# Gated linear attention and merged expert branches on one core: order and due times of attention's last steps, half-column state products, and D parts placed beside the second layer

## The chip, the cores and the metric

The kernel runs on one core of one Trainium2 chip. The metric is device time in microseconds of one execution, from the host's inputs in the chip's memory to the outputs there. Smaller is better.

The engines: TensorE (PE; its weight loads are listed apart as PEld) does matrix products and transposes into PSUM banks. VectorE (DVE) and ScalarE (ACT) do element-wise work and empty the banks. GpSimd (POOL) and SyncE (SP) mainly issue transfers here. Each engine runs its own instructions in the order in which they were recorded.

## What is computed

Two steps follow each other. The first is a recurrent attention, for each of 4 batches and 8 heads over 768 steps, with heads of 48:

```python
for t in range(S):
    state = alpha[:, :, t, :, None] * state + np.einsum('bhd,bhe->bhde', k[:, :, t], v[:, :, t])
    y[:, :, t] = np.einsum('bhd,bhde->bhe', q[:, :, t], state)
```

Its output, laid out as 3072 rows of 384, is the input of four expert branches whose results are weighted by normalised probabilities and added:

```python
p = domain_probs / (domain_probs.sum(-1, keepdims=True) + 1e-09)
for e in range(E):                       # E = 4, D = 384, F = 1024
    h = np.maximum(x @ w1[e], 0.0)
    out += p[:, e:e + 1] * (h @ w2[e])
```

All inputs and outputs are float32.

## The kernel before

**Units and groups.** Attention is cut into 24 units: a chunk of 128 time steps (`cb`, six of them) of one batch (`b`, four). Units are collected in groups for the experts: a first group of 2, five of 4, and a last of 2. A group of four is 512 rows of `x`. For each group and expert, the first layer (`up`, eight tiles of hidden units) and then the second (`down`, 128 rows of output a slot) are done. The last two groups take turns expert by expert.

**Precision.** TensorE multiplies float32 slowly, and a rounded form (float32r) faster. From the second group on the first layer, and from the third on both layers, numbers are split into a top part, a low part and a third part that corrects for products of the two. For the hidden layer these are made by `hidden_parts`: ScalarE makes `top`, VectorE `low` (L571), and `make_dif` (L581) the third, called the D part here. Before the change, the D part of a full group's tile is made half at once, in the first layer (columns 0 to 255), and half later: the list `later` is emptied, one piece at every fourth matmul, in the next `down`. The last group's D parts, of 256 columns, all go to `later`.

**The second layer's order.** `down` takes two slots at a time (a half, 48 matmuls). Top and low parts are multiplied first for six tiles, then for the last two, and then the D parts of all eight tiles, slot by slot: matmuls 32 to 47. Partial sums are added to `acc` by VectorE (L649), or ScalarE for the first expert.

**Attention's steps.** `attention(u)` is a generator; each `yield` ends a step. Steps 0 to 2 turn alpha, keys and queries (`tp`) and load those of the next unit. Steps 3 to 10 run down seven levels: `copy_q` (ScalarE copies queries into a block `qb`), `next_q` and `next_k` (decays multiplied on, VectorE). Step 7 has the products of levels 0 to 3 (`sc`, 64 by 64 tiles), whose scores are taken into `near` by masked copies (`take`). Step 11 has the products across a chunk (`far`) and levels 4 and 5. Steps 12 and 13 copy `far` and `near` into `lat` (ScalarE). Then, before the change: step 14 the result (`yps`, tiles of 32 columns, values times `lat` plus queries times the state) copied out for the experts; step 15 the keys turned and copied (`AT`, used as `KB`); step 16 the state products (`sps`), added to the state by VectorE. Units of the last chunk have no keys to turn and no state to keep.

**Order.** The schedule is written by hand: the kernel records experts' work in order, and `advance` adds up planned costs (`cost`) after each tile or matmul. `deal` gives each step of each unit a due time on this planned clock; when the clock passes it, the step is recorded there. A unit is spread over two spaces, so that two units overlap; before the change its 17 steps are equally spaced:

```python
events += [(begin + (end - begin) * (j + 1) / BEATS, u, run) for j in range(BEATS)]
```

A group's units must be done `MARGIN` ahead of its first use. The first two units are placed by lists written out.

**Buffers that matter.** PSUM: tag `w` (turns, yps, sps) and tag `sc` (scores, far) have two buffers each, tag `g` (both layers' sums) four. `near` and `lat` are single tiles that all units share. Four blocks `qb` go round. `dec6`, a decay used in the update of the state, has one buffer.

Of the kernel before, what the change touches and what calls it, by code (L numbers as in the profile page):

```python
# [10 lines left out]
F32 = mybir.dt.float32  # L11
# [9 lines left out]
def kernel(  # L21
# [37 lines left out]
    nc = tc.nc  # L59
# [79 lines left out]
    splitting = []  # L139
    stores = deque()  # L140
    late = deque()
    later = deque()
    shared = {}
    accs = {}

    BEATS = 17
    MARGIN = 6.0
    waiting = deque()
    clock = 0.0
# [118 lines left out]
    def attention(u):  # L268
# [41 lines left out]
        def next_q(li):  # L310
            m = LEVELS[li]
            qv = halves(QT, m)[:, :, :, 1, :]
            dv = halved(decs[li])
            nc.vector.tensor_mul(qv, qv, spread(dv[:, :, :, 0], m))  # L314
            dec = work.tile([P, NP, P // (2 * m)], F32, name=f"dec{li}", bufs=1)
            nc.vector.tensor_mul(dec, dv[:, :, :, 0], dv[:, :, :, 1])
            decs.append(dec)

# [90 lines left out]
        st = sts[b]  # L409
        flat_st = st.rearrange("p a i d -> p a (i d)")  # L410
        flat_v = rv.rearrange("p (a i) d -> p a (i d)", i=2)
        yps = ps.tile([P, KC, P], F32, name="yps", tag="w")
        for c in range(KC):


            if c < 2:
                now = [[(2 * c + j // 2, j % 2, (0, HD + TAIL)[j % 2], 2 * QUAD * (j % 2))
                        for j in range(4)]]
                turns = ([(True, now[0])] if cb > 0 else []) + [(False, now[0])]
            else:  # L420
                turns = [(True, [(p, 0, 0, QUAD) for p in range(NP)])] if cb > 0 else []
                turns += [(False, [(p, i, QUAD + TAIL * i, 0) for p in range(NP)]) for i in range(2)]
            for n, (past, turn) in enumerate(turns):
                for j, (p, i, in_v, in_st) in enumerate(turn):
                    nc.tensor.matmul(  # L425
                        yps[QUAD * j:QUAD * (j + 1), c, :],
                        lhsT=flat_st[:, p, in_st:in_st + QUAD] if past
                        else flat_v[:, p, in_v:in_v + QUAD],
                        rhs=QT[:, p, :] if past else lat[:, 2 * p + i, :],
                        start=(n == 0), stop=(n == len(turns) - 1))  # L430
        gi, slot = place[cb, b]
        if slot == 0:
            if gi == 0:
                xTs[gi] = work.tile([P, 3, KC, NT], F32R, name="xT", bufs=1)
                xraws[gi] = xTs[gi][:, 2].bitcast(F32)
            elif gi < LAST:
                xraws[gi] = work.tile([P, KC, NT], F32, name="x_raw", bufs=1)
            else:
                xraws[gi] = []
        if gi < LAST:  # L440
            nc.scalar.copy(out=xraws[gi][:, :, slot * P:(slot + 1) * P], in_=yps)
        else:

            xraws[gi].append(AT)
            nc.scalar.copy(out=AT[:, :KC, :], in_=yps)
        yield

        if cb < NCB - 1:
            KB = AT
            nc.scalar.copy(out=KB, in_=turned(lambda p: KT[:, p, :]))  # L450
            yield
            sps = ps.tile([P, NP, 2, D], F32, name="sps", tag="w")
            for p in range(NP):
                nc.tensor.matmul(sps[:, p], lhsT=KB[:, p, :], rhs=rv[:, 2 * p:2 * p + 2, :D],  # L454
                                 start=True, stop=True)
            for i in range(2):
                rows = slice(HD * i, HD * (i + 1))
                old, add = st[rows, :, i, :], sps[rows, :, i, :]
                if cb == 0:
                    nc.vector.tensor_copy(out=old, in_=add)  # L460
                else:
                    nc.vector.tensor_mul(old, old, decs[-1][rows].broadcast_to([HD, NP, D]))
                    nc.vector.tensor_add(old, old, add)
# [103 lines left out]
    def hidden_parts(x, parts):  # L567
        top, low, dif = parts
        nc.scalar.activation(out=top, in_=x, func=ACT.Relu, scale=TRIM)  # L569
        yield  # L570
        nc.vector.scalar_tensor_tensor(out=low, in0=x, scalar=0.0, in1=top.bitcast(F32),  # L571
                                       op0=ALU.max, op1=ALU.subtract)

        n = x.shape[-1]
        at = n // 2 if n == NT else 0
        if at:
            make_dif(*(part[:, :at] for part in parts))
        later.append([part[:, at:] for part in parts])

    def make_dif(top, low, dif):  # L580
        nc.vector.scalar_tensor_tensor(out=dif, in0=top.bitcast(F32), scalar=1 / 4096.0,  # L581
# [6 lines left out]
    def down(gi, e, slots, between):  # L588


        first = first_piece(gi, e)
        halves_ = split2(gi, e)
        if slots[0] == 0 and makes[1](gi, e):
            making.extend(split_piece(1, first + k) for k in range(NQ))
        if slots[0] == 0 and makes[0](gi, e) and 0 < e < E - 1:
            making.extend(split_piece(0, first + k) for k in range(2, NQ))
        sums = [[ps.tile([P, DM], F32, name=f"ops{j}", tag="g", bufs=4)
                 for j in range(2 if halves_ else 1)] for _ in slots]

        kinds = [((0, 1), range(FCH - 2)), ((0, 1), range(FCH - 2, FCH)), ((2,), range(FCH))]  # L600
        steps = [(part, i, fc) for parts, tiles in (kinds if halves_ else [((3,), range(FCH))])
                 for part in parts for i in range(len(slots)) for fc in tiles]
        for n, (part, i, fc) in enumerate(steps):
            c, f = divmod(fc, FPQ)
            h = hidden[c][:, :, f, slots[i] * P:(slots[i] + 1) * P]
            advance(cost(1, gi, e) / FCH / (3 if halves_ else 1))
            while between and n >= between[0][0] * len(steps):
                between.popleft()[1]()
            if n == len(steps) // 2:
                background()  # L610
            if later and n % 4 == 3:
                make_dif(*later.popleft())
            if halves_:
                w = wt[1][first + c].rearrange("p t (c d) -> p t c d", d=DM)[:, part, f]
                nc.tensor.matmul(sums[i][part // 2], lhsT=h[:, part], rhs=w,  # L615
                                 start=(fc == 0 and part != 1), stop=(fc == FCH - 1 and part != 0))
            else:
                w = wt[1][first + c].rearrange("p (c d) -> p c d", d=DM)[:, f]
                nc.tensor.matmul(sums[i][0], lhsT=h[:, 2].bitcast(F32), rhs=w,  # L619
                                 start=(fc == 0), stop=(fc == FCH - 1))  # L620
            if part >= 1 and fc == FCH - 1:
                add_up(gi, e, slots[i], part // 2, sums[i][part // 2 if halves_ else 0])
        while between:
            between.popleft()[1]()
        background()
        if slots[-1] == len(groups[gi]) - 1 and gi != LAST - 1:
            while makes[1](gi, e) and (making or splitting):
                background()

            for c in range(NQ):  # L630
                del wt[1][first + c]
                if c < NQ // 2 or gi == LAST:
                    load_piece(1, first + NQ + c)
                else:
                    late.append(first + NQ + c)
# [31 lines left out]
    def deal():  # L667

        wanted = [0.0]
        ends = [0.0, 0.0]
        events = []
        t = 0.0
        for (gi, e), after in zip(tasks, tasks[1:]):
            part = 1 - 1 / len(groups[0]) if gi == e == 0 else 1
            t += cost(0, gi, e) * FCH * part
            if after[1] == 0:
                wanted.append(t)
            t += cost(1, gi, e) * len(groups[gi]) * part  # L680

        for gis in [*([gi] for gi in range(1, LAST - 1)), [LAST - 1, LAST]]:
            gi, due = gis[0], wanted[gis[-1]] - MARGIN
            n = sum(len(groups[i]) for i in gis)
            first = wanted[gi - 1] if gi > 1 else 0.0
            space = (due - first) / (n if gi > 1 else (n + 1) / 2)
            if gi == 1:
                space /= 2
            for k in range(n):
                u = sum(map(len, groups[:gi])) + k  # L690
                end = due - (n - 1 - k) * space
                begin = max(end - 2 * space, ends[-2])
                ends.append(end)
                run = attention(u)
                events += [(begin + (end - begin) * (j + 1) / BEATS, u, run) for j in range(BEATS)]
        return sorted(events, key=lambda x: x[:2])

    def advance(spent):
# [100 lines left out]
```

## Time and profile before

The table is from the profiled execution and from the runs; the page's names are used.

| | |
|---|---|
| median of 12 runs | 1079.52 us (1077.53 to 1081.02) |
| profiled execution, own time | 1082.44 us |
| its span, first to last instruction | 1080.6 us |
| mean granted TensorE clock | 0.993 |
| L615, second layer's split products | 1728 records, 318.5 us busy |
| L531, first layer's split products (`one`, `two`) | 1728 records, `one` of 512 columns 253.6 us |
| L619, second layer in float32 | 384 records, 135.8 us |
| L581, D parts, 128 by 256 | 288, mean 421 ns |
| L333, level products | 2304 records, 77.6 us |
| L425, result | 768 and 480 records, 34.7 and 25.1 us |
| L454, state products, 128 by 96 | 160 records, 21.0 us |
| HBM traffic | 232 GB/s over the span |

A float32 product appears as two records. Lengths of matmul records overlap each other[...]; what a matmul costs is the distance between starts. "Idle before" and the waits' view name what released an engine that had nothing to do. Busy shares are averages over stages with different limits: the first 170 us work in float32, then the split stages with attention follow to about 890 us, and then the last groups without attention.

### The profile page before, as it was taken

The numbers are of one execution on the slowest core, as the hardware profiler recorded it, in microseconds if no ns is written. First come the engines' busy times: TensorE is split into PE (matmuls) and PEld (weight loads), VectorE is DVE, ScalarE is ACT, GpSimd is POOL, SyncE is SP. The second block draws the span as 40 slices with busy tenths as digits, with TensorE's granted clock in tenths as the row PEclk, the third lists the DMA queues.
The fourth block names the chain that finished last, engine by engine and source line by source line (L and its number), as shares of the span: only waits on it lengthen the run. The fifth ranks groups of instructions, "written<-read, shape, count | busy, mean of one in ns | idle before, by whom it ended". The sixth has DMA issues, their size and how long they took to land.

```text
span 1080.6 us, 21595 instructions
## 1 busy us (share of the span) xinstructions
PE 1055.7 (98%) x8460; PEld 899.5 (83%) x8460; DVE 774.4 (72%) x1711; ACT 566.6 (52%) x1202; POOL 32.8 (3%) x71
## 2 busy tenths in 40 slices
PE   8889899999999999999999999999999999999998
PEld 7766676676767798898898998888989889898988
DVE  5577678556556878777977786986878866666565
ACT  5786766764747555436446445555564543323232
POOL 2000000000000100000000000000000000000000
PEclk9998899999999999999999999999999999999999
DMA  8597679886786968649568568595594643544440
GB/s 124 156 328 220 214 225 379 294 318 239 246 282 214 392 204 324 247 148 358 198 229 319 193 232 317 161 330 220 169 348 146 253 191 128 223 174 177 182 181 33
DMA packets 158838, 251.67 MB, mean 233 GB/s; under 512 B 120112, under 2 KB 135344, under 8 KB 136208
## 3 DMA queue, kind: packets, MB, share of 16 engines
q1 hardware_dynamic: 149600, 208.82, 56.1%
q0 software_dynamic: 5760, 41.29, 9.7%
q8 instruction: 67, 1.10, 0.4%
q10 hardware_dynamic: 3376, 0.17, 0.3%
q14 instruction: 35, 0.29, 0.1%
HBM read 207.79 MB, written 42.47 MB: 232 GB/s over the span
## 4 chain that ended last, share of the span: by engine, by line
PE 81%; DVE 9%; ACT 7%; issue 2%; DMA 1%; SPq 0%; ACTq 0%; DVEq 0%
PE ops L615 26%; PE one L531 21%; PE two L531 10%; PE ops L619 9%; PE sc L333 5%; PE yps L425 4%; PE tp L265 3%; ACT qb L307 2%; PE one L523 2%; PE sps L454 1%; DVE near L343 1%; DVE hT L571 1%; PE far L388 1%; DVE t L544 1%; ACT hT L569 1%
## 5 line engine op out<-in xcount | busy, mean ns | idle before, releaser
L615 PE MATMUL ops<-w,hT 128*128 128x384 f32 x1728 | 318.5, 340 | 2.8 <-DVE acc L649 2.8
L615 PEld LDWEIGHTS ops<-w,hT 128*128 128x128 f32 x1728 | 299.0, 188 | 8.2 <-DVE acc L649 4.1
L531 PE MATMUL one<-xT,w 128*128 128x512 f32 x960 | 253.6, 399 | 0.8 <-DMA w<-kept 0.4
L531 PEld LDWEIGHTS one<-xT,w 128*128 128x128 f32 x960 | 175.9, 188 | 41.8 <-issue 2.4
L542 ACT ACTIVATE t<-one 128x512 f32<-128x512 f32 (+1 forms) x192 | 106.3, 554 | 163.8 <-PE one L531 144.2
L307 ACT COPY qb<-QT 64x256 f32<-64x256 f32 x336 | 136.5, 406 | 72.6 <-DVE QT L288 35.5
L569 ACT ACTIVATE hT<-t 128x512 fp32r<-128x512 f32 (+1 forms) x160 | 94.3, 589 | 111.4 <-DVE t L544 110.2
L571 DVE SCALAR_TENSOR_TENSOR hT<-t,hT 128x512 fp32r<-128x512 f32 (+1 forms) x160 | 102.0, 637 | 60.5 <-ACT hT L569 58.5
L531 PE MATMUL two<-xT,w 128*128 128x512 f32 x480 | 136.3, 392 | 0.0
L619 PE MATMUL ops<-hT 128*128 128x384 f32 x384 | 135.8, 497 | 0.0
L544 DVE TENSOR_TENSOR t<-t,two 128x512 f32<-128x512 f32 (+1 forms) x160 | 100.8, 630 | 39.5 <-ACT t L542 21.1
L581 DVE SCALAR_TENSOR_TENSOR hT<-hT 128x256 fp32r<-128x256 f32 x288 | 112.0, 421 | 4.4
L531 PEld LDWEIGHTS two<-xT,w 128*128 128x128 f32 x480 | 90.2, 188 | 19.9
L619 PEld LDWEIGHTS ops<-hT 128*128 128x128 f32 x384 | 70.1, 192 | 40.5 <-issue 1.6
L343 DVE COPY_PREDICATED near<-masks,sc 128x256 f32<-128x256 uint8 x144 | 77.0, 535 | 19.4 <-PE sc L333 16.4
L314 DVE TENSOR_TENSOR QT<-QT,dec 128x256 f32<-128x256 f32 x144 | 60.7, 421 | 34.4 <-ACT qb L307 34.0
L333 PEld LDWEIGHTS sc<-qb,KT 128*64 128x64 f32 x2304 | 73.3, 139 | 9.2 <-issue 7.1
L333 PE MATMUL sc<-qb,KT 128*64 128x64 f32 x2304 | 77.6, 224 | 0.2 <-ACT qb L307 0.2
L649 DVE SCALAR_TENSOR_TENSOR acc<-ops,p_all,acc 128x384 f32<-128x384 f32 x82 | 49.3, 611 | 29.1 <-PE ops L615 14.2
L326 DVE TENSOR_TENSOR KT<-KT,dec 128x256 f32<-128x256 f32 x144 | 60.1, 418 | 2.8 <-PE tp L265 2.8
L325 ACT COPY KT<-KT 128x256 f32<-128x256 f32 x144 | 59.8, 415 | 3.1
L549 DVE TENSOR_TENSOR hT<-t,two 128x512 f32<-128x512 f32 x32 | 22.0, 688 | 35.5 <-ACT t L542 25.2
(88 smaller groups left out, 972.1 us busy)
## 6 DMA issues: line engine op xcount, KB each, us to landing
w<-kept SPq DMA_DIRECT2D x144, 1152.0 KB
kept<-w POOLq DMA_DIRECT2D x32, 1152.0 KB, 7.7
hT<-in_moe_w_dram SPq DMA_DIRECT2D x32, 384.0 KB
w<-in_moe_w_dram SPq DMA_DIRECT2D x48, 128.0 KB
ra<-in_alpha_dram SPq DMA_DIRECT2D x23, 192.0 KB
rk<-in_k_dram SPq DMA_DIRECT2D x23, 192.0 KB
rq<-in_q_dram SPq DMA_DIRECT2D x23, 192.0 KB
out_dram<-acc POOLq DMA_DIRECT2D x18, 192.0 KB, 6.6
```

Source lines behind the costliest of these rows:

```text
L307: nc.scalar.copy(out=qb[rows, :, i, :].rearrange("p a (b r) -> p a b r", r=m), in_=qv[rows])
L314: nc.vector.tensor_mul(qv, qv, spread(dv[:, :, :, 0], m))
L333: nc.tensor.matmul(out[HALF * s:HALF * (s + 1), 2 * p:2 * p + 2, :], lhsT=KTs[li][:, p, HALF * s:HALF * (s + 1)], rhs=qbs[li][:, p, :, QUA ...
L343: nc.vector.copy_predicated(near.rearrange("p a (b two r) -> p a b two r", two=2, r=m)[:, :, :, 1, :], mk.unsqueeze(1).broadcast_to([P, H, ...
L531: nc.tensor.matmul(out, lhsT=w[:, part, kc], rhs=x_part(gi, part, kc), start=(part == terms[0] and kc == 0), stop=(part == terms[-1] and k ...
L542: nc.scalar.activation(out=t, in_=one, func=ACT.Copy, scale=FINE)
L544: nc.vector.tensor_add(t, t, two)
L569: nc.scalar.activation(out=top, in_=x, func=ACT.Relu, scale=TRIM)
L571: nc.vector.scalar_tensor_tensor(out=low, in0=x, scalar=0.0, in1=top.bitcast(F32), op0=ALU.max, op1=ALU.subtract)
L581: nc.vector.scalar_tensor_tensor(out=dif, in0=top.bitcast(F32), scalar=1 / 4096.0, in1=low.bitcast(F32), op0=ALU.mult, op1=ALU.subtract)
L615: nc.tensor.matmul(sums[i][part // 2], lhsT=h[:, part], rhs=w, start=(fc == 0 and part != 1), stop=(fc == FCH - 1 and part != 0))
L619: nc.tensor.matmul(sums[i][0], lhsT=h[:, 2].bitcast(F32), rhs=w, start=(fc == 0), stop=(fc == FCH - 1))
```

## The change

Six things are changed, all in recording order or tile shape; the computed values are the same sums.

1. Due times are no longer equally spaced: a list `BEATS` for the first ten units, `IN_PAIRS` for units 10 to 23. In `BEATS`, `far` and the result are due a longer while behind the copies they use.
2. For units 10 to 23 (`pairs`), `TOGETHER` sets a unit's step 7 (level products) to the due time of the previous unit's step 15, and its step 11 to that of the previous unit's step 16. Two further rules keep steps 6 and 12 behind the previous unit's steps 13 and 15.
3. From the third unit on, the keys are turned (step 14) before the result (step 15).
4. Where the next unit is in pairs (`apart_`), state products are two of 64 columns by 48 a pair of heads, instead of one of 128 columns by 96 of which half was used.
5. All D parts go to the second layer: `later` becomes two lists, for the first and second half of the slots, each emptied in its own half.
6. `dec6` gets two buffers, and groups 3 and 4 begin `MARGIN` earlier.

```diff
-    BEATS = 17
+    BEATS = [*(0.055 * (j + 1) for j in range(11)), 0.69, 0.75, 0.8, 0.87, 0.94, 1.0]
+    IN_PAIRS = [*(0.0425 * (j + 1) for j in range(8)), 0.385, 0.43, 0.475, 0.52, 0.6, 0.67, 0.755, 0.84, 1.02]
+    TOGETHER = ((15, 7), (16, 11))
+    pairs_from = half + 2 * B
...
-            dec = work.tile([P, NP, P // (2 * m)], F32, name=f"dec{li}", bufs=1)
+            dec = work.tile([P, NP, P // (2 * m)], F32, name=f"dec{li}", bufs=1 + (li == 6))
...
+        def result():
+            yps = ps.tile([P, KC, P], F32, name="yps", tag="w")
...
+        def turn_keys():
+            if cb < NCB - 1:
+                nc.scalar.copy(out=AT, in_=turned(lambda p: KT[:, p, :]))
+
+        for step in (turn_keys, result) if u >= half else (result, turn_keys):
+            step()
+            yield
 
         if cb < NCB - 1:
             KB = AT
-            nc.scalar.copy(out=KB, in_=turned(lambda p: KT[:, p, :]))
-            yield
-            sps = ps.tile([P, NP, 2, D], F32, name="sps", tag="w")
+            apart_ = u + 1 >= pairs_from
+            sps = ps.tile([P, NP, 1 if apart_ else 2, D], F32, name="sps", tag="w")
             for p in range(NP):
-                nc.tensor.matmul(sps[:, p], lhsT=KB[:, p, :], rhs=rv[:, 2 * p:2 * p + 2, :D],
-                                 start=True, stop=True)
+                for i in range(2) if apart_ else [slice(0, 2)]:
+                    rows = slice(HD * i, HD * (i + 1)) if apart_ else slice(0, P)
+                    nc.tensor.matmul(
+                        sps[rows, p], lhsT=KB[:, p, rows],
+                        rhs=rv[:, 2 * p + i, :D] if apart_ else rv[:, 2 * p:2 * p + 2, :D],
+                        start=True, stop=True)
...
-        n = x.shape[-1]
-        at = n // 2 if n == NT else 0
-        if at:
-            make_dif(*(part[:, :at] for part in parts))
-        later.append([part[:, at:] for part in parts])
+        for k in range(0, x.shape[-1], 2 * P):
+            later[k // (2 * P)].append([part[:, k:k + 2 * P] for part in parts])
...
-            if later and n % 4 == 3:
-                make_dif(*later.popleft())
+            dif = later[slots[0] // 2]
+            if dif and n % 4 == 3:
+                make_dif(*dif.popleft())
...
-            first = wanted[gi - 1] if gi > 1 else 0.0
+            first = wanted[gi - 1] - MARGIN * (2 < gi < LAST - 1) if gi > 1 else 0.0
...
-                events += [(begin + (end - begin) * (j + 1) / BEATS, u, run) for j in range(BEATS)]
+                pairs = u >= pairs_from
+                beats = [0.0, *(IN_PAIRS if pairs else BEATS)]
+                due_at = {-1: begin, **{j: begin + (end - begin) * beats[j + 1] for j in (7, 11, 16)}}
+                for ahead, j in TOGETHER if pairs else ():
+                    if (u > pairs_from or j == 11) and abs(times[-1][ahead] - due_at[j]) < space / 6:
+                        due_at[j] = times[-1][ahead]
...
+                for j, ahead in ((6, 13), (12, 15)):
+                    if times[:-1]:
+                        times[-1][j] = max(times[-1][j], times[-2][ahead] + 0.5)
+                events += [(time, u, run) for time in times[-1]]
```

More of the change, by code (lines that the diff above doesn't have):

```diff
@@ L141 @@
     late = deque()
-    later = deque()
+    later = [deque(), deque()]
     shared = {}
     accs = {}
-    BEATS = 17
+    BEATS = [*(0.055 * (j + 1) for j in range(11)), 0.69, 0.75, 0.8, 0.87, 0.94, 1.0]
+    IN_PAIRS = [*(0.0425 * (j + 1) for j in range(8)), 0.385, 0.43, 0.475, 0.52, 0.6, 0.67, 0.755, 0.84, 1.02]
+    TOGETHER = ((15, 7), (16, 11))
+    pairs_from = half + 2 * B
     MARGIN = 6.0
@@ L411, in attention @@
         flat_v = rv.rearrange("p (a i) d -> p a (i d)", i=2)
[L412 to L419, printed above, removed]
-            else:
[L421 to L445, printed above, removed]
@@ L446, in attention @@
-        yield
+        def result():
+            yps = ps.tile([P, KC, P], F32, name="yps", tag="w")
+            for c in range(KC):
+                if c < 2:
+                    now = [[(2 * c + j // 2, j % 2, (0, HD + TAIL)[j % 2], 2 * QUAD * (j % 2))
+                            for j in range(4)]]
+                    turns = ([(True, now[0])] if cb > 0 else []) + [(False, now[0])]
+                else:
+                    turns = [(True, [(p, 0, 0, QUAD) for p in range(NP)])] if cb > 0 else []
+                    turns += [(False, [(p, i, QUAD + TAIL * i, 0) for p in range(NP)]) for i in range(2)]
+                for n, (past, turn) in enumerate(turns):
+                    for j, (p, i, in_v, in_st) in enumerate(turn):
+                        nc.tensor.matmul(
+                            yps[QUAD * j:QUAD * (j + 1), c, :],
+                            lhsT=flat_st[:, p, in_st:in_st + QUAD] if past
+                            else flat_v[:, p, in_v:in_v + QUAD],
+                            rhs=QT[:, p, :] if past else lat[:, 2 * p + i, :],
+                            start=(n == 0), stop=(n == len(turns) - 1))
+            gi, slot = place[cb, b]
+            if slot == 0:
+                if gi == 0:
+                    xTs[gi] = work.tile([P, 3, KC, NT], F32R, name="xT", bufs=1)
+                    xraws[gi] = xTs[gi][:, 2].bitcast(F32)
+                elif gi < LAST:
+                    xraws[gi] = work.tile([P, KC, NT], F32, name="x_raw", bufs=1)
+                else:
+                    xraws[gi] = []
+            if gi < LAST:
+                nc.scalar.copy(out=xraws[gi][:, :, slot * P:(slot + 1) * P], in_=yps)
+            else:
+                xraws[gi].append(AT)
+                nc.scalar.copy(out=AT[:, :KC, :], in_=yps)
@@ L448, in attention @@
+        def turn_keys():
[4 more added lines that the diff above has]
+            yield
         if cb < NCB - 1:
             KB = AT
-            nc.scalar.copy(out=KB, in_=turned(lambda p: KT[:, p, :]))
-            yield
-            sps = ps.tile([P, NP, 2, D], F32, name="sps", tag="w")
+            apart_ = u + 1 >= pairs_from
+            sps = ps.tile([P, NP, 1 if apart_ else 2, D], F32, name="sps", tag="w")
@@ L453, in attention @@
             for p in range(NP):
-                nc.tensor.matmul(sps[:, p], lhsT=KB[:, p, :], rhs=rv[:, 2 * p:2 * p + 2, :D],
-                                 start=True, stop=True)
+                for i in range(2) if apart_ else [slice(0, 2)]:
+                    rows = slice(HD * i, HD * (i + 1)) if apart_ else slice(0, P)
+                    nc.tensor.matmul(
+                        sps[rows, p], lhsT=KB[:, p, rows],
+                        rhs=rv[:, 2 * p + i, :D] if apart_ else rv[:, 2 * p:2 * p + 2, :D],
+                        start=True, stop=True)
@@ L456, in attention @@
             for i in range(2):
                 rows = slice(HD * i, HD * (i + 1))
-                old, add = st[rows, :, i, :], sps[rows, :, i, :]
+                old, add = st[rows, :, i, :], sps[rows, :, 0 if apart_ else i, :]
                 if cb == 0:
@@ L673, in deal @@
         events = []
+        times = []
         t = 0.0
@@ L694, in deal @@
                 run = attention(u)
-                events += [(begin + (end - begin) * (j + 1) / BEATS, u, run) for j in range(BEATS)]
+                pairs = u >= pairs_from
[4 more added lines that the diff above has]
+                        due_at[j] = times[-1][ahead]
+                marks = sorted(due_at)
+                times.append([])
+                for lo, hi in zip(marks, marks[1:]):
+                    times[-1] += [due_at[hi] if j == hi else
+                                  due_at[lo] + (due_at[hi] - due_at[lo]) * (beats[j + 1] - beats[lo + 1])
+                                  / (beats[hi + 1] - beats[lo + 1]) for j in range(lo + 1, hi + 1)]
+                for j, ahead in ((6, 13), (12, 15)):
+                    if times[:-1]:
+                        times[-1][j] = max(times[-1][j], times[-2][ahead] + 0.5)
+                events += [(time, u, run) for time in times[-1]]
         return sorted(events, key=lambda x: x[:2])
```

## The prediction

> **What bounds the kernel now.** I read the busy shares first, then the chain that ended last, TensorE's waits by stretch, and the timeline at the places concerned.
>
> ```profile
> PE 1055.7 (98%) x8460; PEld 899.5 (83%) x8460; DVE 774.4 (72%) x1711; ACT 566.6 (52%) x1202; POOL 32.8 (3%) x71
> ...
> PEclk9998899999999999999999999999999999999999
> ...
> PE 81%; DVE 9%; ACT 7%; issue 2%; DMA 1%; SPq 0%; ACTq 0%; DVEq 0%
> ```
>
> TensorE is busy throughout and carries the chain. A change can only shorten its work, remove its waits, or add to either. Two slices, 81 to 135 us, have a lower clock.
>
> ```profile
> PE yps L425 <- ACT lat L405: 7.7, 5, 3.5
> PE far L388 <- ACT qb L307: 4.6, 4, 1.6
> ```
>
> These are TensorE's two longest waits in the first 150 us. After 150 us there are only two above half a microsecond in sum:
>
> ```profile
> PE ops L615 <- DVE acc L649: 2.8, 4, 1.2
> PE yps L425 <- ACT lat L405: 0.9, 1, 0.9
> ```
>
> The worst early wait in the timeline (start, length, instruction, wait before it):
>
> ```profile
> 121.52 0.43 PE L425 MATMUL yps<-QT,st 128*32 128x128 f32 x8
> 125.44 0.66 PE L425 MATMUL yps<-lat,rv 128*32 128x128 f32 x8 [3.50 <-ACT lat L405]
> 125.87 0.65 PE L425 MATMUL yps<-QT,st 128*32 128x128 f32 x8
> ```
>
> After the wait eight records start 0.43 us apart (125.44 to 125.87). In the fence below they take about 0.22: the wait is followed by half speed.
>
> A steady stretch, TensorE alone:
>
> ```profile
> 656.40 1.54 PE L531 MATMUL one<-xT,w 128*128 128x512 f32 x6
> 657.77 0.85 PE L531 MATMUL two<-xT,w 128*128 128x512 f32 x3
> 658.56 0.42 PE L425 MATMUL yps<-QT,st 128*32 128x128 f32 x8
> 658.80 0.40 PE L425 MATMUL yps<-lat,rv 128*32 128x128 f32 x8
> ...
> 660.22 1.65 PE L531 MATMUL one<-xT,w 128*128 128x512 f32 x6
> 661.71 0.85 PE L531 MATMUL two<-xT,w 128*128 128x512 f32 x3
> ...
> 669.03 1.02 PE L454 MATMUL sps<-rv,AT 128*128 128x96 f32 x8
> 669.84 1.63 PE L531 MATMUL one<-xT,w 128*128 128x512 f32 x6
> 671.31 0.85 PE L531 MATMUL two<-xT,w 128*128 128x512 f32 x3
> ...
> 674.15 2.09 PE L333 MATMUL sc<-qb,KT 128*64 128x64 f32 x64
> 676.17 3.40 PE L615 MATMUL ops<-w,hT 128*128 128x384 f32 x18
> 679.40 0.60 PE L265 MATMUL tp<-ident,ra 128*128 128x128 f32 x4
> ```
>
> Here the cost of a change of array shape (128*128 to 128*32 or 128*64 and back) is read from starts. And the quiet stage without attention, where VectorE's pile after a first layer shows:
>
> ```profile
> 938.85 0.85 PE L531 MATMUL two<-xT,w 128*128 128x512 f32 x3
> 939.54 9.74 PE L615 MATMUL ops<-w,hT 128*128 128x384 f32 x53
> 944.62 2.77 DVE L581 SCALAR_TENSOR_TENSOR hT<-hT 128x256 fp32r<-128x256 f32 x8
> ```
>
> [...] Eight L581 of 0.42 us take 2.77, so one costs (2.77-0.42)/7 = 0.336, its length less 0.083; I take 0.083 off every VectorE length.
>
> **A. Result and products adjacent.** In the changed program's order, 16 of the 24 result blocks (yps) are followed at once by another unit's level products (sc). Each visit to a narrow shape costs an entry and an exit. Entry: `two` starts at 657.77, yps at 658.56, 0.79 later; in the run of `two` to `one` it is 0.69 (655.71 to 656.40): 0.10. Exit of yps: the block has 56 records, 7 times 0.218 = 1.53, but takes 658.56 to 660.22 = 1.66, and the next six `one` take 1.49 instead of 1.37: 0.25. Exit of sc: 64 records at 0.031 (32 of them took 1.03 at 643.76) are 1.98, it takes 2.02, and 18 `ops` then take 3.23 instead of 18 x 0.174 = 3.13 (0.174 from 96 in 16.71 at 1042.54 of the chain): 0.14. Adjacent, yps's exit and sc's entry go, 0.35, and a join comes that no row shows. Bounds: nothing, or the whole 0.35. The nearest row, far to sc, costs 0.05 over its pitch; I take 0.06. 16 x 0.29 = **-4.6** (0 to -5.6).
>
> **B. State products (sps) in half columns.** 11 of 20 units do sixteen records of 64 columns by 48 instead of eight of 128 by 96, ten directly ahead of another unit's far products, whose entry they share. Before: 0.81 plus 0.10 in the next six `one` = 0.91. After: between 16 x 0.021 (far's 0.055 for 128, by columns) = 0.33 and 16 x 0.031 (sc's pitch) = 0.50, and a join of 0.05; I take the slow end, 0.55. 10 x 0.36, and 0.17 for the lone one (0.50+0.10+0.14): **-3.8** (-2.5 to -5.7). The accumulation into the state stays on VectorE, 4 x 0.35 us a unit.
>
> **C. The early waits.** From the third unit on, the keys are turned ahead of the result, and result stands two steps behind the copies of `lat`: by the planner 3.2 instead of 1.35 us behind them in the first group of four, with a turn of 0.36 us between. The yps waits are 2.74 (80 us), 0.97 (101 us), 3.50 (125 us). Less about 2.2 each, they leave 0.5, 0 and 1.3: 5.4 saved. Far's step goes from 1.35 to 1.9 behind its copy; its waits of 1.23 and 0.38 lose 0.5 and 0.38, but steps before are 7% denser, so I count nothing. The half speed after the waits at 80 and 125 us costs about 1.2 in the excess of the rows listed there and 1.7 of `ops` at 0.64 instead of 0.32, and 0.8 and 1.3 in the yps blocks: 5. Half goes: 2.6. **-8** (-3, if ScalarE's queue moves the wait elsewhere, to -12).
>
> **D. Late waits.** acc, 2.8 in four waits, came from VectorE's pile after the first layer (next step). These and the lone yps wait of 0.86: **-3.6** (-2 to -4).
>
> **E. D parts beside the second layer.** As many instructions as before (288), but in the full groups eight of sixteen per expert move from the first layer to the second's first half (slots 0, 1), and the other eight to its second half. VectorE's loop in the first layer was 2.445 us a tile (L581 to L581, 939.73 to 942.18: t, wait for ScalarE, low, D) against TensorE's 2.07 (starts of `one`, 935.42 to 937.48). Without D it is 2.11. The pile of eight times 0.37 = 3 us goes. But now the D part for tile k is issued before matmul 4k+3 and needed by 32+k of the same 48. The last has eight matmuls, 1.4 us.
> Measured on before: had they been needed so, in the first halves with attention the worst D part would have come 1.2 to 3.6 us late, all but one of twelve; sum 24.
> For after I added, half by half, VectorE's work from the last `low` to the last D part, by the program's order and rows' lengths less 0.083. It starts 2.2 us after the first matmul (939.70 end of `two`, then 0.68+0.63+0.69 and two gaps of 0.03, against 939.54). TensorE reaches matmul 39 after 39 x 0.174 = 6.8 plus attention between. Typical (first full group, third expert): eight D, one acc, seven of attention are 5.8; 2.2+5.8 = 8.0 against 7.2 (one turn inside): 0.8 late. Worst (fourth group, third expert): fourteen of attention, 7.3; 9.5 against 6.8: 2.7. Over all: six first halves 0.2 to 1.1, one 2.7, and one second half, where a state update and level products meet, 1.6; together **+8.3**. Low end +2, since VectorE fills its 0.7 us gaps of the first layer with attention; high end +29, if the pile stays as in before (24 with attention, 5 without).
>
> **F. Denser steps at the end.** In the last six units a copy is 2.3 instead of 3.1 us (planner) ahead of its products. The products there started 0.05, 0.46 and 0.33 us after their copies (units 19, 21, 23), else over 1. One microsecond less gives **+1.5** (0 to 4). In the middle units the slack was 3 to 4 us: nothing.
>
> Without effect: the second dec6 buffer (no wait named it); SP's issues move with their steps, at an unchanged distance of a unit (about 41 us) from use; POOL's stay. The chain of state updates has more time than before.
>
> **Sum.** -4.6-3.8-8-3.6+8.3+1.5 = -10.2. The profiled execution took 1082.44 (span 1080.6 and 1.8 around it), so 1072.2 for it; it lies 2.9 above the median of the runs, 1079.52, hence **1069.3**.
>
> **Rivals.**
> 1. VectorE keeps up (E at +2 or less). For it: 72% busy, and free gaps in the first layer. Against: the tally above. -20+2+1.5 = -16.5: 1063.
> 2. Little gained: ScalarE's queue is what is late early (ACT is at 6 to 7 tenths there), so C gives -3, and joins cost more, A -2.5, B -2.5, D -2; +8.3+1.5: about 0, 1079.
> 3. Slower: D parts late in nearly every half of the second layer. It needs VectorE's backlog at the first layer's end to be what it was: bursts of state update and two takes (4 x 0.27 + 2 x 0.45 + 0.34 = 2.3 us at once) behind tile 5 of the first layer would restore it. Then E is 29: +9 to +11, 1089. It decides from E = 22, some 0.9 us for each of 26 halves with attention.
>
> **Chances.** A measurement of this kernel tells about 0.2% (2.2 us). Forecast 0.45, rival 1 0.20, rival 2 0.15, rival 3 0.20. Rival 2 lies mostly within 0.2%, a part under. Faster 0.70, same 0.11, slower 0.19. Range 1060 to 1083: from all gains at their far end to the lower part of rival 3; it leaves out about 0.15 above and 0.05 below. The forecast's own is 1064 to 1075.
>
> **What would show it.** A and B: yps rows followed by sc, `sps` of sixteen in about 0.5 us, TensorE's busy time some 8 us lower. C: yps waits before 150 us near 2, and the two slices of PEclk at 9. D: no wait of ops on acc. E: a new wait of ops on hT by the D line, 8 us in sum; over 20 it would sink the forecast. F: far and sc waiting for qb after 690 us.

## The result and the profile after

The changed kernel takes **1088.1 us** (median of 11 runs, 1084.84 to 1089.38) against 1080.03 for the kernel before (47 runs). The ratio is 1.0072, interval 1.0064 to 1.0081: slower by 7 to 9 us, where 1069.3 was forecast. The time lies above the forecast's range. It went the way of its third rival, though for less than that rival's sum.

The two profiled executions stand closer together than the medians: 1086.51 after, 1082.44 before. The one of before is 2.4 us above its kernel's median, the one of after 1.6 below. The spans differ by 4.1 us, and that is what the traces can explain.

From the page of the changed kernel, busy shares and granted clock:

```profile
PE 1050.5 (97%) x8548; PEld 893.7 (82%) x8548; DVE 769.2 (71%) x1711; ACT 570.6 (53%) x1202; POOL 32.8 (3%) x71
...
PEclk9999999999999999999999999999999999999999
```

TensorE is busy 5.2 us less, and the two slow slices are gone. Part of this is luck: in the profile of before the granted clock was half (0.50) for 13.6 us in these slices (79.7 to 86.5 and 124.0 to 130.8 us), in e2 and e6 below, whose early part is the same program, for 6.8 and 3.4 us only (mean granted clock of the executions 0.997 and 0.998, against 0.993). The span of the changed kernel is longer all the same, so TensorE waits more. Its waits by what released them (total, number, longest), in the first 150 us of the changed kernel:

```profile
PE yps L433 <- ACT lat L411: 3.1, 4, 1.5
PE far L394 <- ACT qb L313: 3.0, 2, 1.6
PE sc L339 <- ACT qb L313: 2.6, 3, 1.2
```

And after 150 us:

```profile
PE ops L632 <- DVE hT L597: 11.8, 16, 2.6
PE far L394 <- DVE hT L590: 2.7, 1, 2.7
PE one L550 <- DVE xT L253: 1.7, 1, 1.7
PE far L394 <- ACT qb L313: 1.2, 1, 1.2
```

Early, the result waits 3.1 us instead of 7.7 and far 3.0 instead of 4.6, with 2.6 us of new waits for level products. Later the four waits on acc and the lone wait of the result are gone, and a new row stands in their place: `ops`, the second layer, waits 16 times for L597, the D parts. The idle time shown is 11.8 us. From start to start of the matmuls around each wait, less the usual 0.174, the delay is longer, 15.0 us in sum (0.16 to 0.27 us more at each wait). The matmul after that follows at 0.28 to 0.34 instead of 0.174, too, and with it the sum is 17.0. (The expectations below say 15.7.) The delays told below are with that matmul, where nothing else is said.

Three places show where time was won and lost. The first matmul of the first split layer starts at 164.7 us instead of 173.9, that of the first split second layer at 377.6 instead of 382.1, and the second layer that follows attention's last step ends at 909.6 instead of 905.6. So 9 us are won early, half of them are gone again after the first split layer, where the first `one` waits for its split input and TensorE then runs at half speed (granted clock 0.50 from 166.9 to 170.3 us), and 8.5 us more are lost after it. Of the 9, some are the luck of the profile of before: e2 and e6, with the same early program, reach the first split layer at 171.7 and 170.1 us.

Where the products stand together, the timeline of the changed kernel (TensorE; start, length) shows what the prediction wanted to see:

```profile
392.92 0.42 PE L433 MATMUL yps<-QT,st 128*32 128x128 f32 x8
...
394.03 0.62 PE L433 MATMUL yps<-lat,rv 128*32 128x128 f32 x16
394.58 2.08 PE L339 MATMUL sc<-qb,KT 128*64 128x64 f32 x64
396.60 1.65 PE L632 MATMUL ops<-w,hT 128*128 128x384 f32 x8
```

```profile
409.46 0.86 PE L550 MATMUL two<-xT,w 128*128 128x512 f32 x3
410.25 0.67 PE L471 MATMUL sps<-rv,AT 128*64 128x48 f32 x16
410.75 0.62 PE L394 MATMUL far<-qb,KT 128*64 128x128 f32 x8
```

yps takes 1.66 us up to sc (and within 0.01 of that at all thirteen such places after 250 us), as long as it took up to `one` before: going from one narrow shape (128*32) to another (128*64) cost here what leaving cost. Saved are sc's entry (0.10) and the slow first products after yps (0.11), so 0.21 a pair. sps takes 0.50 us for its sixteen records, as priced at the slow end.

The quiet stage of the changed kernel, the same place as in the prediction:

```profile
943.84 8.46 PE L632 MATMUL ops<-w,hT 128*128 128x384 f32 x47
945.49 0.69 DVE L590 SCALAR_TENSOR_TENSOR hT<-t,hT 128x512 fp32r<-128x512 f32 x1 [0.70 <-ACT hT L588]
946.10 2.43 DVE L597 SCALAR_TENSOR_TENSOR hT<-hT 128x256 fp32r<-128x256 f32 x7
```

VectorE's pile is gone, as foreseen: the D parts begin 2.3 us after the second layer (946.10 against 943.84) instead of 5.1, and no matmul waits. So the new waits need more than the D parts in the queue: attention's instructions, or, as shown further below, the split of the next group's input. The longest wait, all three engines:

```profile
550.27 4.58 PE L632 MATMUL ops<-w,hT 128*128 128x384 f32 x25
...
551.97 1.42 DVE L597 SCALAR_TENSOR_TENSOR hT<-hT 128x256 fp32r<-128x256 f32 x4
553.33 0.58 ACT L664 ACTIVATE acc<-ops,p_fine 128x384 f32<-128x384 f32 x1 [3.54 <-PE ops L632]
...
555.05 0.84 ACT L313 COPY qb<-QT 64x256 f32<-64x256 f32 x2
...
555.93 0.43 DVE L320 TENSOR_TENSOR QT<-QT,AT 128x256 f32<-128x256 f32 x1 [2.54 <-ACT qb L313]
...
556.94 0.42 DVE L597 SCALAR_TENSOR_TENSOR hT<-hT 128x256 fp32r<-128x256 f32 x1
557.41 1.83 PE L632 MATMUL ops<-w,hT 128*128 128x384 f32 x9 [2.56 <-DVE hT L597]
```

Seven D parts are done by 553.4. The eighth, whose inputs are there at 549.40 (end of L590), runs at 556.94: it stands behind a product of attention's (L320), ahead of which VectorE is idle for 2.54 us, waiting for a copy on ScalarE (L313). That copy, whose queries are there at 552.05 (end of L294), stands behind the first expert's sum (L664), which has waited 3.54 us for TensorE's own sums, and behind two copies of `lat` (1.23 us, left out above). Here VectorE has time; its queue is blocked.

### The profile page after: what moved, and what is told of

Same layout as the page of the kernel before. It is cut to its first block, busy times and chain, and to the rows that moved or that the text cites. A ratio compares the mean times of both kernels' runs of the same rounds, so it can differ in the third digit from the quotient of the medians.

```text
span 1084.7 us, 21812 instructions
## 1 busy us (share of the span) xinstructions
PE 1050.5 (97%) x8548; PEld 893.7 (82%) x8548; DVE 769.2 (71%) x1711; ACT 570.6 (53%) x1202; POOL 32.8 (3%) x71
## 5 line engine op out<-in xcount | busy, mean ns | idle before, releaser
L632 PE MATMUL ops<-w,hT 128*128 128x384 f32 x1728 | 319.4, 341 | 11.8 <-DVE hT L597 11.8
L313 ACT COPY qb<-QT 64x256 f32<-64x256 f32 x336 | 136.6, 406 | 53.2 <-DVE QT L320 25.8
L590 DVE SCALAR_TENSOR_TENSOR hT<-t,hT 128x512 fp32r<-128x512 f32 (+1 forms) x160 | 102.0, 637 | 54.3 <-ACT hT L588 52.8
L550 PE MATMUL two<-xT,w 128*128 128x512 f32 x480 | 138.5, 396 | 0.0
L636 PE MATMUL ops<-hT 128*128 128x384 f32 x384 | 133.5, 491 | 0.0
L597 DVE SCALAR_TENSOR_TENSOR hT<-hT 128x256 fp32r<-128x256 f32 x288 | 105.0, 417 | 0.0
L320 DVE TENSOR_TENSOR QT<-QT,dec 128x256 f32<-128x256 f32 x144 | 60.7, 422 | 44.5 <-ACT qb L313 44.0
```

The lines of the kernel that those rows point to most:

```text
L313: nc.scalar.copy(out=qb[rows, :, i, :].rearrange("p a (b r) -> p a b r", r=m), in_=qv[rows])
L550: nc.tensor.matmul(out, lhsT=w[:, part, kc], rhs=x_part(gi, part, kc), start=(part == terms[0] and kc == 0), stop=(part == terms[-1] and k ...
```

## The experiments

All are told with the ratio of their runs to those of the kernel before on the same chip, and its 95% interval.

| kernel | us | ratio | interval |
|---|---|---|---|
| changed kernel | 1088.1 | 1.0072 | 1.0064 to 1.0081 |
| e1 D parts placed as before | 1081.2 | 1.0017 | 1.0011 to 1.0024 |
| e2 kernel before, D parts moved | 1089.18 | 1.0088 | 1.0069 to 1.0107 |
| e3 changed, D at every second matmul | 1071.88 | 0.9930 | 0.9913 to 0.9947 |
| e4 D as before, no pairs | 1076.49 | 0.9962 | 0.9951 to 0.9973 |
| e5 D at every second, no pairs | 1074.71 | 0.9947 | 0.9932 to 0.9962 |
| e6 kernel before, D at every second | 1076.4 | 0.9964 | 0.9950 to 0.9977 |
| e7 e3 with sps of full columns | 1075.23 | 0.9959 | 0.9942 to 0.9975 |
| e8 changed, D at every third | 1076.07 | 0.9955 | 0.9938 to 0.9971 |
| e9 changed, first sums on VectorE | 1088.76 | 1.0086 | 1.0071 to 1.0101 |
| e10 e3 with later far, earlier split | 1068.34 | 0.9904 | 0.9887 to 0.9920 |

**e1: the D parts' place undone.**

```diff
-        for k in range(0, x.shape[-1], 2 * P):
-            later[k // (2 * P)].append([part[:, k:k + 2 * P] for part in parts])
+        n = x.shape[-1]
+        at = n // 2 if n == NT else 0
+        if at:
+            make_dif(*(part[:, :at] for part in parts))
+        later.append([part[:, at:] for part in parts])
```

> The changed kernel with one part undone: half of each full group's D parts is made in the first layer and the other half in the first half of the second, as before the change. If the D parts' place is the cause (their waits are 15.7 us in the changed kernel's trace), the waits of ops on the D line go and VectorE's pile after the first layer returns as 2 to 4 us of waits on acc: 1088 - 15.7 + 3 = 1075 (1072 to 1078), below the kernel before. If the order of attention's steps is the cause (dense steps, bursts), the time stays at 1084 to 1090.

1081.2: neither. The waits for D parts are gone, yet only half of the expected gain came. TensorE's waits after 150 us in e1:

```profile
PE far L394 <- DVE hT L590: 5.1, 1, 5.1
PE ops L634 <- DVE acc L668: 4.6, 7, 1.6
PE far L394 <- ACT qb L313: 2.1, 1, 2.1
```

With the D parts back in the first layer VectorE's pile is back too. It shows as waits on acc (4.6, expected 2 to 4) and in one place as 5.1 us, where the changed kernel waits 2.7: `far` of unit 18, which the pairs' due times put behind the sixth matmul of a second layer. What far waits for there is told under F below. With the new order, D parts in the first layer cost more than they did before.

**e2: only the D parts moved, in the kernel before.**

```diff
+        for k in range(0, x.shape[-1], 2 * P):
+            later[k // (2 * P)].append([part[:, k:k + 2 * P] for part in parts])
...
+            dif = later[slots[0] // 2]
+            if dif and n % 4 == 3:
+                make_dif(*dif.popleft())
```

> The kernel before with this one part of the change: all D parts beside the second layer, attention's steps equally spaced as before. If the place of the D parts costs by itself, waits of ops on the D line come here too, 10 to 16 us, less the 2.8 us of waits on acc: 1088 to 1093. If the D parts only wait because the changed order sets attention's bursts ahead of them, 1077 to 1082.

1089.18, the first case. The wait in e2:

```profile
PE ops L613 <- DVE hT L578: 8.7, 15, 1.4
```

The time fits; the waits, 8.7 us of idle time, are under the 10 to 16 expected. The new order of attention is not needed for them: with equally spaced steps the D parts are late 15 times too. It may add to them (11.8 in the changed kernel).

**e3: the same D parts earlier in the queue.**

```diff
-            if dif and n % 4 == 3:
+            if dif and n % 2 == 1:
```

> The changed kernel with D parts recorded at every second matmul of a half instead of every fourth: the same work on VectorE, all eight recorded by matmul 15 and so ahead of most of attention's instructions. If the D parts are late because they stand behind attention in VectorE's queue, their waits fall from 15.7 to under 4 us: 1076 to 1080. If VectorE has too much to do in the second layer altogether, the waits stay above 10 us or turn up at acc, qb or the next first layer: 1085 to 1090.

1071.88, better than either case: 15.3 us (1.42%, by the ratios) under the changed kernel, about what its waits for D parts cost, and 8 under the kernel before. The waits after 150 us in e3:

```profile
PE far L394 <- DVE hT L590: 2.7, 1, 2.7
PE one L550 <- DVE xT L253: 2.0, 1, 2.0
PE one L550 <- DVE acc L666: 1.7, 2, 0.9
PE far L394 <- ACT qb L313: 1.2, 1, 1.2
```

No D part is waited for any more; 1.7 us of waits on acc by the next first layer are new. VectorE does the same 1711 instructions, busy 768.2 us against 769.2. Two digits of the program decide: where the work stands in the queue, not how much there is.

**e4: what the early part brings alone.**

```diff
-    pairs_from = half + 2 * B
+    pairs_from = 99
```

and the D parts as in e1.

> The changed kernel without pairs (no unit is set together with the next, state products of the old shape, all units on the list of the early units) and with the D parts as before the change. What is left of the change are the keys turned ahead of the result and the later result and far products. If the early waits are a gain, their 7.2 us of yps waits before 150 us fall to about 3: 1074 to 1077. If ScalarE's queue only moves them, 1078 to 1081. Against e1 it shows what pairs and half-column state products bring: by my prices 7 to 8 us, so e1 should lie 4 us or more under e4, if their waits take no more than 3 us back.

1076.49, the first case: what is left of the change is a gain of 4.1 us (2.9 to 5.3). It is the early waits less what came anew after 150 us, 4.2 us of waits on acc (2.8 before) and 2.1 for the split input (0.3 before); all units are on the early units' list here. But e1 does not lie 4 us under e4, it lies 5 above: with the D parts in the first layer, pairs lose more by waits than they win in work.

**e5: the pairs' worth with the D parts in a good place.** e3 with the edit of e4's pairs_from.

> D parts all beside the second layer at every second matmul, no pairs: state products of the old shape and the early units' list of due times for all units. Against e3 (1071.9), which has the pairs. If pairs and half columns are worth 7 to 8 us less the 4 us that far waits for its copies in e3, this takes 1074 to 1076. If pairs are worth nothing on the whole, as e1 against e4 (1081.2 against 1076.5) would have it, 1067 to 1072.

1074.71, the first case. Pairs and half columns together are worth 2.8 us by the medians, 1.8 by the ratios, whose intervals overlap. Of executions with the same mean granted clock, 0.998, e5's take 1075.2 to 1075.3 us and e3's 1071.8 and 1072.0, so the sign is likely, the size between 1.8 and 3.5.

**e6: place and pace of the D parts alone, in the kernel before.** The edit of e2 with `n % 2 == 1`.

> The kernel before with one edit: all D parts beside the second layer, recorded at every second matmul (e2 had every fourth and took 1089.2). If place and pace of the D parts are one thing and the order of attention another, the 8.7 us of waits on the D line in e2 vanish, and so do the 2.8 us of waits on acc of the kernel before: 1075 to 1079. If at equal spacing VectorE is too full in the second layer, 1082 to 1088.

1076.4, the first case. One edit against e2 is worth 13.4 us by the ratios. All D parts beside the second layer are a gain of 3.9 us if they stand early, and a loss of 9.5 if late. Against e5, which adds the early order, it is only 1.8 us slower by the ratios, whose intervals overlap: with the D parts in a good place the early order is worth less than in e4.

**e7: state products of full columns.**

```diff
-            apart_ = u + 1 >= pairs_from
+            apart_ = False
```

> e3 with one edit: state products of 128 columns by 96 again for all units, still next to far. By my price half columns save 3.8 us together with the joint visit of the narrow shape (2.5 to 5.7): 1074.5 to 1077. If they save nothing[...], 1071 to 1073.

1075.23, the first case: half columns are worth 3.1 us by the ratios, whose intervals just overlap (4.4 to 4.7 between the executions at clock 0.998), against a price of 3.8. In its trace the eight records take 0.95 to 0.96 us up to far where e3's sixteen take 0.50. And e7, which has pairs with full columns, is no faster than e5, which has no pairs (1075.23 against 1074.71): what the pairs gain without the half columns, their waits take back.

**e8: between the two paces.** `n % 3 == 2`.

> The changed kernel with D parts at every third matmul: the last is recorded at matmul 23 of a half instead of 31 (e3: 15), so each has 8 matmuls, 1.4 us, more before its use. The waits of the changed kernel are mostly under 1.4 us for one D part; if they come from the place in VectorE's queue, about 3 us of 15.7 remain: 1073 to 1076. If e3 gained by something else than an earlier place, the time is not between e3 and the changed kernel in this proportion (half way, 1080).

1076.07 (0.07 us above the expected range), and the wait in e8 is what the queue's place would leave:

```profile
PE ops L632 <- DVE hT L597: 3.6, 4, 1.2
```

Idle behind D parts falls from 11.8 in 16 waits to 3.6 in 4, and to none in e3, as the last D part goes from matmul 31 to 23 to 15.

**e9: the blocked queue.** The first expert's sums written by VectorE:

```diff
-            nc.scalar.activation(out=acc, in_=part, func=ACT.Copy, scale=scale)
+            nc.vector.tensor_scalar_mul(out=acc, in0=part, scalar1=scale)
```

> The changed kernel with one edit: the first expert's sums are written by VectorE instead of ScalarE, eight of 0.6 us for each full group. In the changed kernel the longest wait for a D part (2.56 us in the profile, at 557) seems to come by way of ScalarE: its sum copy waits 3.54 us for TensorE, attention's qb copy stands behind it, VectorE waits 2.54 us for qb, and the last D part stands behind that. If so, that wait goes and VectorE has no idle time ahead of that D part; the other two waits of first experts (0.6 at 384, 0.8 at 730) are VectorE's work alone and stay or grow: 1084 to 1088. If it was VectorE's amount of work, the wait grows by the sums: 1089 to 1093.

1088.76 in all, between the ranges of the two cases. The same place in the timeline of e9:

```profile
551.97 0.86 ACT L313 COPY qb<-QT 64x256 f32<-64x256 f32 x2 [1.15 <-DVE QT L294]
...
553.74 0.42 DVE L320 TENSOR_TENSOR QT<-QT,AT 128x256 f32<-128x256 f32 x1
...
554.75 0.42 DVE L597 SCALAR_TENSOR_TENSOR hT<-hT 128x256 fp32r<-128x256 f32 x1
...
555.22 4.43 PE L632 MATMUL ops<-w,hT 128*128 128x384 f32 x24 [0.49 <-DVE hT L597]
```

The qb copy is done three microseconds earlier, VectorE is not idle ahead of L320, and TensorE waits 0.49 us instead of 2.56. The chain by way of ScalarE is shown for this wait. The other two of first experts grew with the added work (0.9 to 1.6 at 385, 1.1 to 1.6 at 731 us of the changed kernel) and another D wait came, 0.6, in the half after the longest, so the total stayed about the same.

**e10: an attempt at the best of it.** e3 with

```diff
+                if pairs and (u >= 20 or u == 18):
+                    due_at[11] += 2.0
...
-                    for step, at in enumerate((0.0, 0.52, 0.62, 0.72)):
+                    for step, at in enumerate((0.0, 0.52, 0.62, 0.72) if gi else (0.0, 0.4, 0.5, 0.6)):
```

> e3 with two more edits: far products of units 18 and 20 to 23 due 2 planned us later, and the second group's input split earlier in the last down of the first group (0.4, 0.5, 0.6 instead of 0.52, 0.62, 0.72). e3 still waits 2.7 and 1.2 us with far there, and 2.0 us for the split input with 1.4 us at half speed after it. If these are late copies and a late start, about 5 us go: 1066 to 1069. If they only move, 1070 to 1073.

1068.34, the first case, and the fastest here: 10.4 us under the kernel before (ratio 0.9904). Against e3 it is 2.8 us by the ratios, whose intervals overlap; the two edits are not told apart. Its waits after 150 us:

```profile
PE far L394 <- ACT qb L313: 2.2, 2, 1.9
PE one L550 <- DVE acc L666: 1.7, 2, 0.9
PE one L550 <- DVE t L290: 1.1, 1, 1.1
```

Far's wait at unit 18 is down from 2.7 to 0.3, the wait at the first split `one` from 2.1 to 1.1, and far's wait for qb at unit 23 has grown from 1.2 to 1.9.

## Why the prediction was wrong

The step that failed is **E**, the D parts beside the second layer, priced at +8.3. It had the place and the mechanism, D parts that stand too late in VectorE's queue, but the waits cost 15 to 17 us in the trace, and e3 shows 15.3 of the time hanging on them. The tally of VectorE's work ahead of the last D part was too small, and in two ways.

First, it had one second half late, by 1.6. Four were late, by 7.5 in sum: 0.7 (478 us), 1.8 (521), 3.6 (694 to 698) and 1.4 (872). The last three are those of the fourth expert, in which VectorE also splits the next group's input: six instructions (L253, L254) of 0.68 to 0.69 us, which the prediction names nowhere. All three halves with this work were late; of the nine other second halves only the one at 478 us was, and there VectorE was idle for 2.26 us, waiting for a copy. Around the worst of the three:

```profile
691.86 0.69 DVE L254 SCALAR_TENSOR_TENSOR xT<-xT 128x512 fp32r<-128x512 f32 x1
...
694.01 0.69 DVE L253 TENSOR_TENSOR xT<-x_raw,xT 128x512 fp32r<-128x512 f32 x1
...
694.74 0.69 DVE L254 SCALAR_TENSOR_TENSOR xT<-xT 128x512 fp32r<-128x512 f32 x1
...
697.35 0.41 DVE L597 SCALAR_TENSOR_TENSOR hT<-hT 128x256 fp32r<-128x256 f32 x1
...
697.82 1.83 PE L632 MATMUL ops<-w,hT 128*128 128x384 f32 x9 [1.22 <-DVE hT L597]
```

Second, it left out what VectorE's queue stands still for. All first halves but one were put at 1.1 or less, and the one at 557 us cost 2.8, of which e9 removes most. The stretches that end with the last D part of these two halves (length; then busy time of TensorE, its weight loads, VectorE, ScalarE and GpSimd; then granted clock and DMA) show the difference:

```profile
687.07:697.76 10.69, 8.07 (x44) 7.06 (x43) 10.39 (x26) 4.44 (x11) 1.08 (x2) 1.00 0.17 54
547.40:557.36 9.96, 7.45 (x46) 7.10 (x44) 6.69 (x16) 5.70 (x13) 0.00 (x0) 1.00 0.95 210
```

In the first VectorE is full, in the second it is blocked. The full queue is the larger part of the surplus. That the split of the input fills it is read from the trace; no run moves that split alone, and e3, which sets the D parts ahead of all that follows, does not tell the two ways apart. In its typical case the tally was close (0.8 for the third expert of the first full group; 0.7 in the trace), and in its worst too dark (2.7 against 0.9, at 819 us).

The third rival had the same mechanism with a wrong trigger. It said that VectorE's pile after the first layer would stay. The pile went, as the quiet stage shows; the D parts are late without it, in 12 of the 24 halves up to 875 us, because the last of them has 1.4 us (eight matmuls of 0.174) between record and use.

**C**, the early waits, -8: right in kind, too large. By e4 they bring 4.1 us in time, by e5 against e6 1.8. In the profiles the first 165 us give 9, but three things take from it: a new wait for the split input at 167 us (1.7 us idle, then some 3 us at half speed); 2.6 us of new waits for level products, because the steps before are denser, which I had counted as nothing; and the half speed in the profile of before, 13.6 us long, which I took as typical. That execution was 2.4 us over the median of its kernel.

**A**, -4.6: the term of the join was mis-sized. It is not 0.06 but about 0.14, as much as yps takes at once when the wide shape follows, so 16 x 0.21 = -3.4. In time it does not show: in e7 **F**'s waits are there too, and it is no faster than e5. **B**, -3.8: 3.1 in e7, or a little more. **D**, -3.6: right in the trace, no wait on acc is left.

**F**, +1.5: more. Two waits of far, 2.7 and 1.2 idle, delay TensorE by 4.2 us from start to start. Both are behind a copy as said. At unit 18 the profile names VectorE's L590, which far does not read; the copy of qb, which it reads, ended at 676.75, far started at 676.81, and its weight load names the copy. Far stands there at the start of a second layer, and the copy in ScalarE's queue behind the first layer's last tiles. In e1 the same wait is 5.1.

Taken together: E +7 to +9, C +4 to +6, F +2.7, A +1.2, B up to +0.7 make 15 to 20, around the 18.8 us between forecast and result. No closer account is possible from these runs, as the parts change each other's worth.

The two other rivals fell: VectorE does not keep up at this pace (it does in e3), and the gains were not small. They were covered.

## What to carry to other kernels

When work is moved to a place where another engine uses it soon, add up all the work ahead of it in its queue, also that of a step that comes once in a group, and ask of each instruction ahead what it waits for: here a full queue cost up to 3.6 us in one half, and a blocked one 2.8. Better still, record such work as early as its inputs allow, ahead of work with slack: here the same instructions at every second matmul instead of every fourth made 1071.9 out of 1088.1. And when a change in several parts is slower, look for the part whose waits are new before giving up the rest: the early order and the half columns were gains, and so were the D parts at another pace. The pairs were not shown to be one by themselves.

## What was not expected of the hardware

Half speed after a wait was not a matter of the wait's length alone. In the changed kernel a wait of 1.67 us at 167 us, with 0.46 idle shortly before, was followed by matmuls of 512 columns at 0.43 us instead of 0.23; the granted clock was half from 166.9 to 170.3 us. A wait of 2.56 us (557 us) was followed by full speed (granted clock 1.00 from 557.4 to 565.0 us). And one and the same wait, 2.67 us at unit 18, was followed by full speed in the changed kernel (granted clock 1.00 from 676.8 to 684.0 us) and in e9 by about half speed, after far itself: the 32 products of `sc` take 1.10 us in the first and 1.72 in the second, the seven of `ops` behind them 1.50 and 2.39:

```profile
676.81 0.66 PE L394 MATMUL far<-qb,KT 128*64 128x128 f32 x8 [2.67 <-DVE hT L590]
677.29 1.10 PE L339 MATMUL sc<-qb,KT 128*64 128x64 f32 x32
678.33 1.50 PE L632 MATMUL ops<-w,hT 128*128 128x384 f32 x7
```

```profile
675.13 0.66 PE L394 MATMUL far<-qb,KT 128*64 128x128 f32 x8 [2.67 <-DVE hT L590]
675.62 1.72 PE L339 MATMUL sc<-qb,KT 128*64 128x64 f32 x32
677.27 2.39 PE L632 MATMUL ops<-w,hT 128*128 128x384 f32 x7
```

What decides between the two is not shown by these runs. The price of like waits differed, then, and so did executions of one kernel, with the clock they were granted: on the chip of e1 to e4 the kernel before took 1082.3 and 1082.8 us at a mean granted clock of 0.993, and 1078.1 to 1079.6 at 0.998.

A change between two narrow array shapes (128*32 to 128*64) took as long as one back to the full shape: yps lasts 1.66 us up to `sc` (392.92 to 394.58 in the changed kernel) and up to `one` (658.56 to 660.22 in the kernel before). The profile's idle time understated TensorE's waits here: the sixteen waits for D parts show 11.8 us of idle time, 15.0 from start to start, and 17.0 with the matmul that follows.
